# A delta-rule recurrence with a layer norm and a two-product MLP on one core: chunk 0 in two token halves, and mixed batches in the merged key product

## The chip, the cores and the metric

The kernel runs on one core of a Trainium2 chip. The metric is the device time of one execution in microseconds (us), smaller is better; a profiled execution also gives a trace, whose span runs from the first to the last instruction.

## The reference, cut to what matters

There are 4 batches, 8 heads, 768 tokens and a head size of 48, so the model width is 384, and the MLP is 1536 wide. The weights reach the kernel as 64-bit floats.

```
k_n = k / (norm(k) + 1e-6)
for t in range(768):                      # state is 48x48 for each batch and head
    y[t]  = q[t] @ state
    v_old = state^T @ k_n[t]
    state = state + beta[t] * outer(k_n[t], v[t] - v_old)
x   = y, heads joined: (4, 768, 384)
xn  = (x - mean) / sqrt(var + 1e-6) * g_ln
out = x + relu(xn @ w_ch1) @ w_ch2
```

## The kernel before, in words

**Chunks.** The 768 tokens are worked on in 12 chunks of 64. In a chunk the recurrence becomes a triangular system: G holds the key products K K^T, X is the inverse of a unit triangular matrix made of G and beta, and U = X V (V with the state's part taken off) are the values that are really written. Then y = (masked Q K^T) U + Q S, and the state S grows by K^T U. The inverse is made for blocks of 32 tokens on DVE (`rows_inverse` for pairs of chunks from 2 on, in 31 steps of a product and a subtraction, L1178 and L1185; `rows_near` for chunks 0 and 1, which works on blocks of 16 tokens, L1088 and L1095). For chunks 0 and 1 `near_join` puts two blocks of 16 together into one of 32: a transpose (L1135), a product on PE, a copy with a minus sign on ACT, a second product on PE (both L1140), and a predicated copy into X (L1147). The two blocks of 32 tokens of a chunk are joined in `recur`, by three steps of U on PE (L1256): the diagonal block of the first 32 tokens, the block below it, the diagonal block of the second 32. Between them stand a copy of U on ACT (L1266) and a subtraction on DVE (L1262).

**From y to the MLP.** For chunk 0, y of all 64 tokens is made after the third step (L1271), copied (L1312), its mean and variance taken on DVE (L1318, L1319), normalised (L1345 to L1351), turned on PE (L1383), and multiplied by g (L1399 on ACT, L1389 on DVE). The MLP of a chunk works on 256 rows: 4 batches by 64 tokens. Chunks 0 to 2 make the first product in the plain way: 12 groups (one for each 128 of 1536 columns) of 3 products, each two passes on PE with 256 columns (L1561), then a relu on ACT (L1570). Chunk 0's second product is plain too (L1583). Later chunks use schemes with fewer products: L1492 with 128 columns for the first one, L1664 with 192 for the second one.

**Weights.** Twelve pieces of 768 KB, six for each matrix, come as 64-bit words by DMA on the ACT queue (`fetch`) and are made 32-bit in four steps (`convert`): two on ACT (L798, L806), one on DVE (L803), one on POOL (L816).

**Merged key product.** From chunk 4 on, `gram_queries` makes the key products and the masked query products in one go, in two halves (`gram_half`, L1017), one for each bank pair. Each half has 32 products, two passes each, on array tiles of 64 rows by 32 columns. In a half all heads belong to one batch group g. In the column strip where the token block b equals g a product has 128 columns, in the other strip it has 64. ACT copies the diagonal blocks (L1030, three copies for a half) and the off-diagonal ones (L1042, two copies of 256 columns), and DVE masks the query part (L1035).

**Order.** Nothing runs in the order of the code. Each operation is a step with an engine, a cost, what it reads and writes, and a priority. A planner in the file runs through them and writes out one fixed order for each engine. What steers it are lists of numbers: `DUE` (one start and a slope for the MLP of each chunk or kind), `CAP` (latest times of the inverses), `T0` (earliest times of transfers) and `OFF` (one offset for each part of the program). PE is kept busy early on by products with zeros (L828, L1745).

Of the kernel before, what the change touches and what calls it, by code (L numbers as in the profile page):

```python
# [429 lines left out]
def kernel(  # L430
# [34 lines left out]
    UPER = 0.0076  # L465
    APART = 4
# [56 lines left out]
    pmask = sb("pmask", [128, 2, C])  # L523
# [3 lines left out]
    mask4 = sb("mask4", [128, BK], I32)  # L527
    lane = sb("lane", [128, 6])
# [25 lines left out]
    DUE = [-305.067857599, -184.157488926, 455.196580585, 43.3608971536, 325.931658715, 418.81557092, 734.822875439, 596.087521503, 954.313194593, 1226.15149798, 1753.77174886, 1187.43924725, -1.6924469742, 7.47712706956, 1.31274637377, 1177.34078649]  # L554
    CAP = [747.889715428, 1212.19696458, 1084.81830387, 1850.25080892, 1448.91733639, 908.561376039, 705.970562755, 575.226842462, 821.351411096, 750.46942201, 1687.9172189, 1227.4281115, 847.781737921, 881.489018474, 1102.45793961, 1447.53022967, 1091.57755388]
    T0 = [32.9830988769, 43.9377940451, 29.0921020937, 44.9281472705, 63.7206388166, 107.721780452, 109.01717894, 42.4201425188, 137.327678312, 9.9371017997, 7.55135349446, 21.1072922972, 47.3695615515, 3.2653345546, 12.003557196, 58.3820362978, 9.11313409582, 34.3183793157, 80.7294725245, 31.0940483985, 65.2240956281, 73.1210354066, 26.5270080195, 53.6799046277, 66.9289646085, 120.165225966]
    OFF = [-61.6829581914, -49.2365532767, -61.5532218662, 17.9216944294, -8.93066007944, -19.7935657519, -0.868007026628, 0, 8.96654600389, -13.8380038365, -50.331393939, -0.246849623501, -27.4676130541, 7.77550058171, -22.6886143688, -3.86879544818, -821.586638896, -2.38324144815, -18.1419009006, 5.55478119707, -0.273775179226, -4.22332705522, 80.7687098368, -5.39747372829, -20.4523790178, 62.9055142488, -7.43344176114, 31.9790263038, 21.8074958819, 8.7032008021, 8.84329072182, -13.4908722439, -14.3458640854, -21.0142536144, -8.17343430205, -9.08488196034, 3.21270803936, 29.7501729987, -370.210698155, 9.64783740174, -54.0771745917, 0, 6.02876528764, -18.715620035, -0.0266946289401, -157.574112514, 0.282239804554, -7.26929256528, -11.082495992, -8.27251668698, 6.02892269239, -13.9072145046, 0.152204562562, 22.7850900002, -47.5224937959, -1.16466857269, 2.33155240109, -49.6486518684, -51.2601416133, -62.465549245, -258.793504219, 1.2326483113, 35.4487428898, 31.3088385871, 11.2699410861, -113.147994473, 15.6085619425, -5.03125681565, -202.178096924, -25.0752772067, -0.665071753919, -6.77933533358, 3.23511675889, -68.4395072164, -60.5873923385, -42.4358792875, -97.9842212258, 12.0160900273, 18.6777945201, -900.573997296, -391.422008629, -20.8554491287, 12.9662458348, 1.75202460465, -24.9412070649, 4.97794129872, 75.9129714421, 9.69658805447, 5.43644995158, -526.886362328, -23.7620747742, 4.87077107518, 20.8620167161, 22.9095302211, -1.446032994, -2.31148664706, -2.833545276, 55.9003753723, 63.1638387207, -218.31594106, 287.768221191, 39.9673797514, 0, 804.43668455, 12.7893706811, 40.0678037528, 191.615596099, 0, 7.62314549532, 0, 51.2829387214, 28.4043993347, -5.30420927608, 18.5190140875, -7.64728420003, 7.63987656771, 61.2399462693, 717.489554984, 104.850886777, -30.443334038, -17.6796729001, 1.15630637025, 33.0836625929, 44.5914396091, 124.896962022, 76.2257084997, -17.2048186859, 9.19876963592, 11.8954016929, 17.6790867831, 26.5462796852, 8.59903556167, 24.5744786777, 48.2415672492, 84.1439987925, 573.112593574, -0.31404467451, 2.58380493428, 8.06139582684, -33.4691328586, -35.9526386931, -3.41549753963, 12.8997354829, -1.70472339012, -86.5639462817, 30.2317600188, 0.770084801705, 4.89412762855, 18.4175254922, -4.62459749441, -11.6877931109, 15.5755669109, -4.74496253875, 7.29402960805, -3.92469752656, -16.6201385477, -20.5867367042, 28.2665321084, 4.92853485667, 0, 15.3621971178, -8.42832996846, -56.587083905, 4.72501651567, -56.0564350712, -36.0703739182, 29.6200097296, 32.9003356762, -13.8377451749, 27.2835896047, -1.24739066499, 8.93640941449, 3.28676443186, 297.478212758, -19.9986109974, 45.0956057028, 0, -23.0001510965, 0, 36.6024183436, -9.30579353749, 11.8322652961, 15.1603515043, -21.1764521199, -3.23342658561, 10.9691701204, 0, -53.330288128, -6.9355981517, 35.7517193679, 17.1361544279, -16.5818223692, 7.98946302238, -5.9600414049, 135.238583305, 43.2173490845, 35.7070773331, 1504.57932506, -1.37439939367, 2.80197877523, 83.3684246786, -142.866519066, -50.2056045983, 97.2746589799, 0.00958371475404, 1.62790837443, -2.01014429694, 1.24356061286, 12.6149232043, -4.38744746062, -11.0164345418, -23.3392998149, -60.6068970653, -10.8042936204, -38.5434794118, 2.00080739243, -2.74074762392, -5.2820291742, -29.0236507323, 43.1273234385, 0.946905692554, -24.3700937813, 0, -21.7407793415, -12.5188513858, -23.5560537382, -50.7954370929, -3.45193559535, 15.4383131463, -11.5511037154, 16.3023360558, -25.1832177565, 16.2211956562, 10.4191918731]
# [102 lines left out]
    )  # L660
    SMALL = ["xor", "bits", "ma", "mb", "mc"]

    c_pool(lambda: nc.gpsimd.memset(pmask, 1.0), 0.2, ["pmask"])
    for e in range(2):
        c_pool(
            lambda e=e: nc.gpsimd.affine_select(
                out=pmask[half(e), 0], in_=pmask[half(e), 0], compare_op=ALU.is_gt, fill=0.0, base=0,
                pattern=[[1, C]], channel_multiplier=-1,
            ),
            0.3, ["pmask"],  # L670
        )
    for x in range(4):
        c_pool(
            lambda x=x: nc.gpsimd.affine_select(
                out=pmask[quad(x), 1], in_=pmask[quad(x), 1], compare_op=ALU.is_gt, fill=0.0, base=BK * (x % 2 - 1),
                pattern=[[1, C]], channel_multiplier=-1,
            ),
            0.3, ["pmask1"], r=["pmask"],
        )
# [317 lines left out]
    def gram_half(c, g, ps, pk, **kw):  # L997
# [5 lines left out]

        def segs(ap, step, n):
            return bass.AP(tensor=ap.tensor, offset=ap.offset, ap=[ap.ap[0], [step, 2], [1, n]])

        def prod():
            for j in range(NP):
                for hp, e in hp_e:
# [412 lines left out]
    def cap(i):  # L1422
        return CAP[i]

# [467 lines left out]
```

## Time and profile before

| what | us |
|---|---|
| runs shown | 531.07, 531.5, 535.16 (median 531.5) |
| the profiled execution | 531.07 |
| its span | 529.2 |
| PE busy | 501.5 (95% of the span) |
| DVE busy | 369.4 (70%) |
| POOL busy | 211.3 (40%) |
| ACT busy | 196.7 (37%) |

The profiled execution's own time is 1.9 us above its span. PE is the engine with the least idle time. The times of lines below are from the profiled execution; some records of matmuls are missing, so that a half of a merged product shows as, say, 39 of its 64 passes.

### The profile page before, as it was taken

The page shows a single profiled execution, that of the slowest core. Times are in us where ns is not written, and L with a number is a line of the kernel's source. Part 1 is how long each engine was busy: PE and PEld are TensorE (multiplying, and loading weights), DVE is VectorE, ACT ScalarE, POOL GpSimd, SP SyncE. Part 2 cuts the span into 40 slices and gives each one's busy share as a digit, 9 for nine tenths or more (in the row PEclk, how much of TensorE's full clock was granted, in tenths as well). Part 3 has the DMA queues.
Part 4 walks back from the last instruction along what each step waited for, and adds up shares of the span by engine and source line. Part 5 has one row for each costly group of instructions (what it writes and reads, how often), then busy time and mean ns, then how long its engine had stood idle before and what let it go on. Part 6 is the DMA issues. An engine that isn't in the chain of part 4 may idle for free.

```text
span 529.2 us, 22198 instructions
## 1 busy us (share of the span) xinstructions
PE 501.5 (95%) x9706; PEld 455.5 (86%) x9706; DVE 369.4 (70%) x849; ACT 196.7 (37%) x420; POOL 211.3 (40%) x320
## 2 busy tenths in 40 slices
PE   5967799999999999999999989999999999999996
PEld 3746677768898999989999879999889999999995
DVE  1899559997399866889895589895688893452331
ACT  2834875513812623525204522513523213242030
POOL 6151422236333560642724242452351815235352
PEclk8576779999999999999999999999999999999999
DMA  9965544365645445455311435221233010221101
GB/s 156 281 140 122 86 129 130 94 93 86 86 67 84 90 81 81 94 75 115 59 31 19 67 86 92 51 61 33 58 70 91 1 30 5 63 62 29 31 2 30
DMA packets 157457, 40.53 MB, mean 77 GB/s; under 512 B 150816, under 2 KB 153888, under 8 KB 157360
## 3 DMA queue, kind: packets, MB, share of 16 engines
q1 hardware_dynamic: 153520, 29.40, 31.4%
q10 hardware_dynamic: 3552, 9.63, 5.7%
q8 instruction: 76, 1.25, 1.0%
q0 software_dynamic: 288, 0.07, 0.1%
q14 instruction: 21, 0.17, 0.1%
HBM read 30.82 MB, written 8.26 MB: 74 GB/s over the span
## 4 chain that ended last, share of the span: by engine, by line
PE 86%; DVE 6%; issue 2%; DMA 2%; ACT 2%; SPq 1%; POOL 0%; DVEq 0%; ACTq 0%
PE f L1664 28%; PE f L1492 25%; PE f L1561 10%; PE two L1256 4%; PE f L1583 3%; PE by L1216 2%; PE two L1216 2%; PE by L1271 2%; PE two L1281 2%; PE two L1017 2%; DMA kr<-in_k_dram 1%; PE f L1140 1%; SPq L599 1%; DVE tmp L1088 1%; PE by L1017 1%
## 5 line engine op out<-in xcount | busy, mean ns | idle before, releaser
L1650 POOL TENSOR_TENSOR h_all<-h_all 128x256 f32<-128x256 f32 x99 | 73.9, 751 | 79.1 <-PE f L1664 65.9
L1664 PE MATMUL f<-w_sb,h_all 128*128 128x192 f32 x396 | 97.1, 333 | 1.4 <-ACT xln L1336 0.8
L1664 PE MATMUL f<-words,h_all 128*128 128x192 f32 x396 | 90.1, 329 | 0.0
L1492 PE MATMUL f<-xnt,w_sb 128*128 128x128 f32 x648 | 87.1, 277 | 0.4 <-issue 0.4
L1492 PEld LDWEIGHTS f<-xnt,w_sb 128*128 128x128 f32 x648 | 80.0, 192 | 1.6 <-ACT xnt L1377 0.9
L1664 PEld LDWEIGHTS f<-w_sb,h_all 128*128 128x128 f32 x396 | 66.3, 190 | 5.1 <-issue 2.3
L1515 DVE TENSOR_TENSOR h_all<-f,h_all 128x512 f32<-128x512 f32 (+1 forms) x90 | 49.5, 555 | 28.9 <-PE f L1492 19.8
L1664 PEld LDWEIGHTS f<-words,h_all 128*128 128x128 f32 x396 | 67.6, 190 | 1.1 <-ACT xln L1336 0.2
L1689 POOL TENSOR_TENSOR words<-h_all 128x128 f32<-128x128 f32 x66 | 32.8, 515 | 86.0 <-ACT h_all L1512 76.4
L1185 DVE TENSOR_TENSOR xb<-xb,tmp 128x31 f32<-128x31 f32 (+15 forms) x155 | 61.3, 396 | 4.0
L1178 DVE TENSOR_TENSOR tmp<-xb,gb 128x31 f32<-128x31 f32 (+15 forms) x155 | 60.0, 387 | 5.2 <-POOL xb L1164 1.0
L1561 PE MATMUL f<-xnt,w_sb 128*128 128x256 f32 x216 | 54.6, 399 | 1.2 <-issue 1.2
L1561 PEld LDWEIGHTS f<-xnt,w_sb 128*128 128x128 f32 x216 | 41.5, 198 | 8.2 <-issue 1.7
L1266 ACT COPY u<-two 128x768 f32<-128x768 f32 x24 | 19.2, 800 | 51.3 <-PE two L1256 43.8
L1492 PE MATMUL f<-second,w_sb 128*128 128x128 f32 x216 | 33.1, 276 | 1.7 <-POOL second L1472 1.7
L1512 ACT ACTIVATE h_all<-f 128x512 f32<-128x512 f32 (+1 forms) x36 | 17.4, 489 | 42.7 <-PE f L1492 31.0
L1682 DVE TENSOR_TENSOR o<-f,x 128x192 f32<-128x192 f32 x33 | 11.6, 352 | 30.5 <-PE f L1664 22.7
L1664 PE MATMUL f<-w_sb,words 128*128 128x192 f32 x132 | 32.1, 328 | 0.0
L1570 ACT ACTIVATE h_all<-f 128x256 f32<-128x256 f32 x36 | 13.7, 384 | 49.2 <-PE f L1561 49.0
L1492 PEld LDWEIGHTS f<-second,w_sb 128*128 128x128 f32 x216 | 29.2, 192 | 2.0 <-POOL second L1472 2.0
L1512 ACT ACTIVATE h_all<-h_all 128x512 f32<-128x512 f32 (+1 forms) x36 | 18.7, 521 | 29.4 <-DVE h_all L1515 29.3
L856 POOL TENSOR_TENSOR v<-v,knrms 128x768 f32<-128x768 f32 x10 | 15.3, 1533 | 30.4 <-PE f L1561 11.4
(194 smaller groups left out, 858.6 us busy)
## 6 DMA issues: line engine op xcount, KB each, us to landing
words<-in_moe_w_ch_dram ACTq DMA_DIRECT2D x8, 768.0 KB
out_dram<-o SPq DMA_DIRECT2D x48, 96.0 KB
xld<-xlt SPq DMA_DIRECT2D x9, 384.0 KB
xnt<-xld SPq DMA_DIRECT2D x36, 96.0 KB
tb<-in_q_dram SPq DMA_DIRECT2D x40, 64.0 KB
tb<-in_k_dram SPq DMA_DIRECT2D x32, 64.0 KB
v<-in_v_dram SPq DMA_DIRECT2D x8, 192.0 KB
w_sb<-in_moe_w_ch_dram ACTq DMA_DIRECT2D x2, 768.0 KB
```

Source lines behind the costliest of these rows:

```text
L1178: lambda j=j, n=n, w=w, t=t: nc.vector.tensor_tensor(out=t, in0=xb[:, 0:n, j : j + 1].to_broadcast([128, n, w]), in1=gb[:, j : j + 1, j + ...
L1185: "DVE", dve(n * w), lambda t=t, rest=rest: nc.vector.tensor_tensor(out=rest, in0=rest, in1=t, op=ALU.subtract),
L1216: nc.tensor.matmul(dst[half(e), hp, j], src[drows(hp), (e if n else key_half(c, hp, e)) * GP + j], s_all[drows(hp), e, j], start=(n == 0 o ...
L1256: nc.tensor.matmul(*args(e, e ^ hp, 2 * j + hp))
L1266: add("ACT", act(768), lambda: nc.scalar.copy(u_j, p_2), TWO, uk, after=["nought", *SMALL] if not c else (), **kw)
L1492: nc.tensor.matmul(wide(p[:, o : o + 128]), w[:, f : f + 128], r, start=start and m == n == 0, stop=stop, skip_group_check=True)
L1512: add("ACT", act(128 * m), lambda: nc.scalar.activation(to[0], p, ACTF.Relu), pk, to[1])
L1515: add("DVE", dve(128 * m), lambda v=ps(p): nc.vector.tensor_tensor(out=to[0], in0=v, in1=y[0], op=op), [*pk, *y[1]], to[1])
L1561: nc.tensor.matmul(p[:, 0:TOK], w1_sb[:, t, f * 128 : (f + 1) * 128], xnt[:, t], start=(t == 0), stop=(t == KC - 1))
L1650: add(eng, cost, lambda: e.tensor_tensor(out=out_, in0=x, in1=y, op=op), r, w, port=2 if eng == "Pool" else 1, pr=-2)
L1664: lambda f=f, t=start and f == 0: nc.tensor.matmul(p[:, 0:D2], lhs(f), rhs[:, f], start=t, stop=(f == F2 - 1), skip_group_check=True),
L1689: lambda f=f + i: e.tensor_tensor(out=s3[f], in0=one(0, 0)[0](f), in1=one(1, 0)[0](f), op=ALU.subtract),
```

## The change

Four things are changed, and two masks are added for them.

1. *Chunk 0 by token halves.* `near_join(0)` runs twice, once for tokens 0 to 31 and once for tokens 32 to 63, each with half of the passes and a mask of its own; the first goes to bank f2, the second to f3. After the first step of U and its copy, y is made from what U holds by then (`y0`), and the whole of the norm, now in a function `normed`, runs on it into the buffers of index 1 (x, statistics, normalised and turned rows), which hold right values for tokens 0 to 31. The recurrence goes on as before, and at its end y, norm and turn run again for all tokens into the buffers of index 0.
2. *First product of chunk 0 by token halves* (`first_mlp`): 12 groups for tokens 0 to 31 (from index 1), then 12 for tokens 32 to 63 (from index 0), each with 128 columns instead of 12 groups with 256. The relus are halved likewise.
3. *Mixed batches in the merged key product.* A half now takes both batch groups and half of the heads of each, so that products of 128 and of 64 columns meet in every column strip. Their number and sizes stay. The copies of the off-diagonal blocks become four of 128 columns for a half instead of two of 256.
4. *New order.* `DUE`, `CAP`, `T0` and `OFF` are all replaced, and the planner's own cost for a half of the merged product is lowered.

```
-        pe(128, lambda: prod(pe_, gf, xn, BK), ...
-        add("ACT", act(512), lambda: nc.scalar.mul(es, pe_, -1.0), FK[2], [ek], **kw)
-        pe(128, lambda: prod(pz_, es, xt), [ek, ("xd", c)], FK[2], 0.22, per=0.009, **kw)
+        for b in range(1 if c else 2):
+            quads = range(4) if c else (b, b + 2)
+            if b:
+                line.part += 1
+                pe_ = pz_ = f_[3].rearrange("p (h t) -> p h t", t=BK)
...
+            np, per = (128, 0.009) if c else (64, 0.0165)
...
+            if not c and not n:
+                line.part += 1
+                pe(64, lambda: out_y(range(GP)), [("pt", 0), *uk], BY, 0.65, name="y0", **kp_e)
+                normed(1, [(p_y, BY)] * 2, **kw)
+                line.part += 1
...
+    def first_mlp(n):
+        line.part += 1
+        for f in range(FT):
+            p, pk = bank()
+
+            def parts(t, n=n):
+                return t.rearrange("p (g i b) -> p g i b", g=2, b=BK)[:, :, n::2]
+
+            def first(f=f, p=p, n=n):
+                o = p[:, 0:128].rearrange("p (g i b) -> p g i b", g=2, b=BK)
+                for t in range(KC):
+                    nc.tensor.matmul(
+                        o, w1_sb[:, t, f * 128 : (f + 1) * 128], parts(xnts[1 - n][:, t], n), start=(t == 0), stop=(t == KC - 1)
+                    )
...
-            for j in range(NP):
-                for hp, e in hp_e:
-                    lk, lq = (((2 * x + g) * NP + j) * C for x in (key_half(c, hp, e), e))
-                    for b in range(2):
-                        o = ps[quad(2 * (e ^ hp) + b), hp, j * 2 * C : (j + 1) * 2 * C]
-                        if b == g:
+            for j in range(HP):
+                for r in range(2):
+                    for hp, e in hp_e:
+                        lk, lq = (((2 * x + r) * NP + HP * j + g) * C for x in (key_half(c, hp, e), e))
+                        for b in range(2):
+                            at = (r * HP + j) * 2 * C
+                            o = ps[quad(2 * (e ^ hp) + b), hp, at : at + 2 * C]
+                            if b == r:
...
         for e in range(2):
-            o, w = jn(goff[quad(2 * e + g), i])[:, :, hs], v[quad(2 * e + g), :, :, BK * (1 - g) : BK * (2 - g)]
-            add("ACT", act(256), lambda o=o, w=w: nc.scalar.copy(o, w), pk, [("go", i, e, x, g) for x in range(2)], **kw)
+            for r in range(2):
+                o = mine(jn(goff[quad(2 * e + r), i]))[:, :, HP * r : HP * r + HP]
+                w = v[quad(2 * e + r), :, HP * r : HP * r + HP, BK * (1 - r) : BK * (2 - r)]
+                add("ACT", act(128), lambda o=o, w=w: nc.scalar.copy(o, w), pk, [("go", i, e, x, r) for x in range(2)], **kw)
```

Of the earliest times (`T0`, rounded to whole numbers, in the planner's own us), these concern the front: the six pieces of the first weight matrix 8, 21, 47 (columns 0 to 767) and 3, 12, 58 (columns 768 to 1535) before, 29, 9, 25 and 1, 1, 42 after; the keys of chunk 2 44 before, 4 after; the values of chunk 1 29 before, 67 after; the queries of chunk 1 10 before, 48 after.

More of the change, by code (lines that the diff above doesn't have):

```diff
@@ L527 @@
     mask4 = sb("mask4", [128, BK], I32)
+    masks = [sb(f"mask{b}", [128, BK], I32) for b in range(2)]
     lane = sb("lane", [128, 6])
@@ L660 @@
     )
+    c_dve(
+        lambda: nc.vector.tensor_tensor(out=masks[1], in0=mask4, in1=mc, op=ALU.mult), 0.2, [("mask", 1)], ["mask4", "mc"], port=1,
+    )
+    c_dve(
+        lambda: nc.vector.tensor_tensor(out=masks[0], in0=mask4, in1=masks[1], op=ALU.subtract), 0.2, [("mask", 0)],
+        ["mask4", ("mask", 1)], port=1,
+    )
     SMALL = ["xor", "bits", "ma", "mb", "mc"]
@@ L1404, in recur @@
+        normed(c % 2, pys, **kw)
         if not c:
@@ L1553, in mlp @@
             return seven(c, hs, 33 * 0.43)
-        for f in range(FT):
+        if not c:
+            hs = list(range(FT))
+            first_mlp(1)
+        for f in range(FT) if c else ():
             p, pk = bank()
```

314 lines of the change are left out of this document (172 added, 142 removed).

## The prediction

> **What bounds the kernel now.** I read the busy shares first, then the table of stretches (start:end, length, busy us of PE, weight loads, DVE, ACT, POOL, then granted clock, DMA share, GB/s), then the chain that ended last, and last the rows of the lines that change.
>
> ```profile
> PE 501.5 (95%) x9706; PEld 455.5 (86%) x9706; DVE 369.4 (70%) x849; ACT 196.7 (37%) x420; POOL 211.3 (40%) x320
> ...
> PEclk8576779999999999999999999999999999999999
> ```
>
> ```profile
> 38.70:46.39 7.69, 4.40 (x133) 2.92 (x132) 7.00 (x27) 3.19 (x4) 1.79 (x2) 0.74 0.35 63
> 46.39:67.31 20.92, 16.32 (x544) 14.85 (x545) 13.24 (x31) 15.67 (x29) 7.05 (x7) 0.66 0.57 109
> 67.31:524.40 457.09, 452.05 (x8466) 416.47 (x8465) 323.01 (x706) 159.95 (x355) 184.91 (x277) 0.99 0.33 65
> ```
>
> From 67.31 on PE is busy for 452.05 of 457.09 us at full clock: after the front, time is PE work plus 5.0 us of gaps. Only two things can shorten it: less PE work, or an earlier start of the full stretch. Before 67.31 PE has gaps and a low clock. The chain shows what it does there:
>
> ```profile
> ...
> 56.60 2.15 issue
> ...
> 60.21 1.71 PE two L896 x62
> 62.15 0.88 issue
> 63.03 1.93 PE f L1140 x94
> 64.96 1.15 PE f L1561 x2
> 66.11 1.20 issue
> 67.31 4.42 PE f L1561 x10
> ...
> 81.40 0.81 PE two L1256 x64
> ...
> 130.49 1.07 PE two L1017 x39
> ...
> 399.27 13.40 PE f L1492 x120
> ...
> ```
>
> Two rows of PE's timeline (start, length, passes) stand for what the chain hides:
>
> ```profile
> 47.28 1.07 PE L1271 MATMUL by<-u,pt 64*64 64x48 f32 x32
> 48.14 1.92 PE L1281 MATMUL two<-u,kr 64*64 64x48 f32 x64
> ```
>
> The first product of the MLP (L1561) begins at 64.96, though chunk 0's rows were ready at 53.86 (L1389, 53.30 + 0.56). They came late, so their weights were left late too: the last early piece was issued on ACT's queue at 48.90 and its L816 ended at 60.89, 12.0 us later. What is to be seen is how slow PE is here: 10 passes of L1561 take 4.42 us, 0.442 each, where later 6 take 1.29 (0.2155 each); L1281 takes 1.92 and later 0.89.
>
> **Part 1 and 2, the front.** *When are the rows of tokens 0 to 31 ready?* U of the first step is copied by 39.57 (L1266, 38.77 + 0.80). `y0` has as many passes as both L1271 pieces, 1.11 + 1.07 = 2.2, so 41.8. From the first copy of y (47.57) to the last rows (53.86) it now takes 6.3 us. That gives 48.1, against 64.96 for the first L1561. Half joins cannot bring it much earlier: each array tile gets as many passes as before.
>
> *Are the weights there?* The columns needed first come from three pieces whose earliest times go from 8, 21, 47 to 29, 9, 25; the last of them by the 12.0 us above is ready at about 41. Price: the ACT queue now issues two other pieces at the start, beside the SP queue's keys of chunk 0 (landing 9.15, on the chain) and the keys of chunk 2, moved from 44 to 4. DMA is already full at 10 to 30 us (share 1.07 to 1.13). I take nothing for it, since 7 us lie between 41 and 48.1; if the landing at 9.15 itself slips, all of it counts, and I bound that by 3 us, about a third of its 7.5 us.
>
> *What is gained?* The 12 half groups are 72 passes of 128 columns: 72 x 13.40/120 = 8.0 us of PE work that can be done before the point that is now 67.31. Is there room? Idle is 20.92 - 16.32 = 4.6. Low clock costs, against the same counts later: two L896 about 0.7 each (against 1.08 of L1216), L1281 1.0, L1140 0.7 (against 1.22 at 55.13), the first two L1561 0.7, together 3.8; and 4.42 - 10 x 0.2155 = 2.3 behind 67.31. Room 10.7. New work in it: `y0` again, at full clock 0.94 (L1271 later), and six turns, 2 x 0.33 (L1383), 1.6 together. So 9.6 of 10.7 is used, and the start moves by 8.0 - 1.6 = **6.4**. Bounds: 0 (the start doesn't move) and 10.7 - 1.6 = 9.1.
>
> *Halving costs* 24 x 3 x 2 x 0.1117 = 16.08 against 72 x 0.2155 = 15.52: **+0.6**.
>
> *DVE* gets two norms (0.56 + 0.18 + 0.15 + 0.48 each), one L1389 (0.56), one L1147 (0.73) and two masks (0.24 each): 4.5 us where it is busy for 14.9 of 16.0 us (30 to 46). What goes back is `rows_near(1)`, whose steps end at 50.57, and with it the join of chunk 1. Its cover is 65.73 (L1147) to 81.40 (chunk 1's U): 15.7 us. Nothing is charged; without the cover it is 4.5.
>
> *ACT* gets two copies (0.48), two roots (0.29), three L1399 (0.37), one L1143 (0.60) and, for the first half, 12 relus (0.38, as L1030 for 128 columns): 7.8 us. In 46.39 to 67.31 it has 15.67 of 20.92, so 23.5 would be 2.6 too many. The conversions L798 and L806 at 56.88 to 58.74, four of 0.55, can go into the stretch before (ACT 3.19 of 7.69): 2.2 less. I charge **+0.4**. The relus are what empties the two banks in which half groups stand, so a relu behind the eight copies L907 (1.03 each) makes PE wait.
>
> The turn of `normed` is a wait added on PE: behind it stand the second join and two steps of U, and for them the rest of chunk 0. PE has fill products (L1745) there now, so up to the 1.2 + 0.7 us of these is covered.
>
> **Part 3, the merged product.** A half has 64 passes on 8 array tiles. At 13.40/120/128 = 0.87 ns a column, a tile in the busier strip works 8 x 128 columns = 0.89 us, in the other 0.45. The rows give about 1.0 for a half (1.07 above). Mixed, each tile has 4 x 128 + 4 x 64 columns, 0.67. With the same 0.11 on top it is 0.78, so 0.22 less for each of 16 halves: **-3.5**, and all of it counts since PE is 99% busy there. Bounds: 0.73 for a half, the shortest row for 64 small passes (L1256 from chunk 4 on), gives -4.3; 1.08, the longest (L1216), +1.3. I take -3.5, as the load of the tile is what changes.
>
> The Trainium skill speaks against this: "TensorE: Matmul & The Clock Gate", section "Wait — 56ns, not 53.3ns?", says that matmuls never start closer than about 25 ns apart, however short they are. By that, 64 passes would take 1.6 us in any mix and the part would bring nothing. The trace disagrees: the row of L1256 has 64 passes in 0.81 us, 12.7 ns each, so I give this little weight; with no gain here the sum would be 525.6.
>
> ACT pays for the mix: four copies L1042 more for a chunk at 0.37, 1.5 us, 11.8 over 8 chunks. ACT works 160 of 457 us there, and its copies (to 302.5 in the pair at 296) stand ahead of an inverse that is used later. Charged at nothing; without cover, 3.0 for a pair, four pairs 12.
>
> **Part 4, the new order.** No row prices it. Gaps of PE behind 67.31 are 5.0 us now. I bound it by -3 (2 us of gaps stay) and +15.8 (rival C), and take 0, as DVE (323 of 457) and ACT have room.
>
> **Sum** against the profiled execution: 531.07 - 6.4 + 0.6 + 0.4 - 3.5 = **522.2**; the median of the runs is 531.5, 0.4 above it. About 1% (5.3 us) is what a measurement can tell from no change here.
>
> **Rivals.** *A, the front keeps its start*: ACT or the banks hold the half groups back, or the order runs them only behind 67.31. For it speak ACT's 23.5 of 20.92 and the low clock; against it the free 5 to 8 us in the stretches before. PE then pays 1.6 + 0.6 and gains 3.5: 529.8.
>
> *B, the mix brings nothing*: passes are bound by something other than the tile. For it: L1216, with four tiles and 48 columns, takes 1.08 though its tiles work only 0.67. Against: L1256. 522.2 + 3.5 = 525.7.
>
> *C, slower: a chunk's rows come late.* From chunk 3 on, rows go from L1336 through DVE, out and back by DMA on SP's queue, and ACT to L1492. Now 298.46 to 314.21 is such a trip, 15.8 us, and PE idles only 2.6 in that stretch, as it has other products. `DUE` of chunk 1 goes to 806, so other products may be used up earlier. From 8.9 us uncovered the gains are eaten; a whole trip bare gives 522.2 + 15.8 = 538.0. Against it: one trip in nine shows, and for 1.7 us.
>
> *D, more than the sum*: the whole room is used, the mix reaches 0.73 and gaps shrink by 3: 531.07 - 9.1 + 0.6 - 4.3 - 3 = 515.3.
>
> **How the numbers follow.** Forecast 0.47 (its own range 518 to 526), A 0.15, B 0.11, C 0.16, D 0.11. Faster by over 1% means under 525.8 (526.2 from the median): nearly all of the forecast (0.46), D (0.11), half of B (0.05): 0.62. Slower by over 1%: C from 14 us bare, 0.15 of it. The rest, 0.23, is within 1%. The range goes from 513, below D by the 2 us of gaps that are left, to 535, which takes in A, B, a late first landing (525) and the lower half of C; some 0.12 of C and a little of D lie outside.
>
> **What would show it.** First product of chunk 0 starting at 47 to 52 and PE without gaps from about 61; clock full from there; L1017 0.75 to 0.85 for a half, 12.5 for all where it is 16; PE's gaps behind the front still about 5. The forecast is wrong if the first product starts late or stands in gaps behind relus, if a half stays at 1.0, or if a wait on rows (L1377's successors, POOL, ACT's L1336) over 5 us shows on PE.

## The result, and the profile after

The changed kernel takes 537.65 us in the median (534.65 to 540.36, 10 runs), the kernel before 531.29 us on the same chip (527.68 to 536.39, 10 runs): ratio 1.0124, 95% interval 1.0087 to 1.0161. The ratio leaves out one slow run of the kernel before (536.39 us). The forecast was 522.2, with a range of 513 to 535 and 0.62 for faster. Sign and range are wrong. The profiled execution after took 538.11 us (span 536.4), 7.0 us more than the one before. A second batch of runs on another chip gave 537.39 us and a ratio of 1.0159 (1.0131 to 1.0187). The experiments below ran on several chips; each one's ratio is to the kernel before on its own chip, and is read against this 1.0159.

The page of the kernel after (busy us, share, instructions):

```profile
PE 504.8 (94%) x9840; PEld 459.1 (86%) x9840; DVE 374.6 (70%) x861; ACT 203.6 (38%) x472; POOL 214.9 (40%) x320
```

The table of stretches after, at two of the bounds that the prediction used (start:end, length, busy us of PE, weight loads, DVE, ACT, POOL, granted clock, DMA share, GB/s):

```profile
46.39:67.31 20.92, 18.24 (x402) 15.75 (x400) 17.80 (x64) 16.73 (x35) 7.20 (x6) 0.84 0.82 191
67.31:524.40 457.09, 445.56 (x8711) 411.13 (x8710) 324.87 (x704) 164.79 (x398) 183.22 (x273) 0.99 0.31 59
```

No pass is missing from these two traces: the merged product has 1024 in each, 16 halves of 64, and a row of the chain with 39 shows a part of a half. The 134 passes that the kernel after has more are the second y (64), six turns and the halves (72), less eight fill passes.

Ahead of 67.31 PE now looks better: 18.24 busy of 20.92 (16.32 before) and clock 0.84 (0.66). Behind it, 11.5 us are gaps (5.0 before). The chain of work that ended last shows what stands there now; copies on ACT and the join of chunk 1 are in it where the kernel before had PE's first product:

```profile
38.06 1.69 PE f L1163 x58
39.91 1.16 PE two L1396 x56
...
64.29 1.03 ACT gdiag L923
...
72.77 1.93 PE f L1163 x128
```

PE's timeline after has the same events, from `y0` to the start of the early half, and at the join (start, length, passes, idle time before and what ended it):

```profile
42.94 2.04 PE L1286 MATMUL by<-u,pt 64*64 64x48 f32 x64
...
49.53 1.50 PE L1396 MATMUL two<-v,xt 32*32 32x48 f32 x64 [2.68 <-DVE v L1402]
...
55.95 1.11 PE L1418 MATMUL two<-u,kr 64*64 64x48 f32 x64
56.99 2.30 PE L1594 MATMUL f<-xnt,w_sb 128*128 128x128 f32 x18
...
72.77 1.93 PE L1163 MATMUL f<-xt,pt 32*32 32x32 f32 x128 [2.86 <-ACT pt L1177]
74.63 4.21 PE L1594 MATMUL f<-xnt,w_sb 128*128 128x128 f32 x18
```

The early half of the first product begins at 56.99, not at 48.1. At 72.77 PE waits 2.86 us inside chunk 1's join, and then 18 passes take 4.21 us, 0.234 each; at 87.95, with the clock at 1.00, 24 such passes take 2.94, 0.122 each.

The waits of PE that the profile lists from 46 to 92 us come to 6.4 us after, all of them for DVE or ACT. Before they came to 5.5 us, and 4.2 of these were the three gaps that the prediction's chain shows as "issue" (2.15, 0.88, 1.20), where the profile names nothing that PE waited for. So waits for data grew from 1.3 to 6.4 us.

**Where the 7 us stand.** To compare the two traces over time I gave every PE pass the spacing that its kind has at clock 1.00 (0.112 us for 128 columns, 0.216 for 256, 0.163 for L1664 and L1734, 0.0127 for a pass of U, and so on) and summed what was still to be done at a given time. The table shows how much more the kernel after has left than the kernel before, in us, in both of its profiled runs.

| time, us | 30 | 70 | 80 | 200 | 240 | 260 | 280 | 400 | end |
|---|---|---|---|---|---|---|---|---|---|
| after | 2.2 | -1.6 | 2.7 | 5.1 | 5.1 | 8.8 | 9.8 | 5.4 | 7.2 |
| after, second run | 2.2 | -0.7 | 3.5 | 7.3 | 7.3 | 9.3 | 10.4 | 5.4 | 6.8 |

The 2.2 at 30 us is the added work (y twice, six turns, the halves), as forecast (1.6 + 0.6). At 70 us the early half has put PE ahead. Between 70 and 80 that is lost, between 240 and 260 2 to 4 us more, and from 280 to 400 some come back. The ten runs of the kernel after lie 5.7 us apart, so a row of a single execution is read for its place, not for its last us.

### The profile page after: what moved, and what is told of

The parts are those of the page before. It is cut to its first block, busy times and chain, and to the rows that moved or that the text cites. A ratio compares the mean times of both kernels' runs of the same rounds, so it can differ in the third digit from the quotient of the medians.

```text
span 536.4 us, 22520 instructions
## 1 busy us (share of the span) xinstructions
PE 504.8 (94%) x9840; PEld 459.1 (86%) x9840; DVE 374.6 (70%) x861; ACT 203.6 (38%) x472; POOL 214.9 (40%) x320
## 4 chain that ended last, share of the span: by engine, by line
PE 63%; DVE 18%; SPq 6%; ACT 5%; DMA 4%; issue 3%; POOL 1%; DVEq 0%; ACTq 0%; POOLq 0%
PE f L1533 23%; PE f L1734 23%; SPq L601 6%; DVE tmp L1212 4%; DVE xb L1219 4%; PE two L1396 4%; DMA kr<-in_k_dram 2%; PE by L1250 2%; PE f L1163 2%; PE f L1631 2%; ACT gdiag L923 2%; PE two L1250 1%; PE by L1286 1%; DVE kq L892 1%; PE two L1418 1%
## 5 line engine op out<-in xcount | busy, mean ns | idle before, releaser
L1734 PE MATMUL f<-w_sb,h_all 128*128 128x192 f32 x396 | 96.9, 333 | 0.6 <-DVE o L1752 0.5
L1734 PE MATMUL f<-words,h_all 128*128 128x192 f32 x396 | 87.4, 328 | 0.1
L1759 POOL TENSOR_TENSOR words<-h_all 128x128 f32<-128x128 f32 x66 | 31.5, 494 | 139.4 <-ACT h_all L1553 100.4
L1533 PEld LDWEIGHTS f<-xnt,w_sb 128*128 128x128 f32 x648 | 80.5, 192 | 5.8 <-ACT xnt L1361 4.3
L1734 PEld LDWEIGHTS f<-w_sb,h_all 128*128 128x128 f32 x396 | 66.0, 190 | 3.5 <-issue 1.4
L1734 PEld LDWEIGHTS f<-words,h_all 128*128 128x128 f32 x396 | 67.6, 190 | 1.0 <-ACT h_all L1553 0.3
L1212 DVE TENSOR_TENSOR tmp<-xb,gb 128x31 f32<-128x31 f32 (+15 forms) x155 | 61.2, 395 | 4.1
L1219 DVE TENSOR_TENSOR xb<-xb,tmp 128x31 f32<-128x31 f32 (+15 forms) x155 | 60.4, 390 | 4.0
L1631 PE MATMUL f<-xnt,w_sb 128*128 128x256 f32 x144 | 35.6, 387 | 0.3 <-ACT h_all L1640 0.3
L1734 PE MATMUL f<-w_sb,words 128*128 128x192 f32 x132 | 32.5, 332 | 0.1
L1631 PEld LDWEIGHTS f<-xnt,w_sb 128*128 128x128 f32 x144 | 26.2, 190 | 4.9 <-ACT h_all L1640 1.0
L1752 POOL TENSOR_TENSOR o<-o,words 128x192 f32<-128x192 f32 x22 | 13.3, 622 | 36.6 <-DVE words L1752 29.2
L892 DVE STREAM_TRANSPOSE kq<-tb 128x256 f32<-128x256 f32 (+2 forms) x34 | 23.3, 718 | 5.7 <-DMA tb<-in_q_dram 3.7
L1752 DVE TENSOR_TENSOR o<-f,x 128x192 f32<-128x192 f32 x33 | 11.6, 350 | 22.3 <-PE f L1734 18.8
```

Source lines behind the costliest of these rows:

```text
L892: "DVE", 0.18 + 1.035e-3 * n, lambda o=o, w=w: nc.vector.transpose(o, w), tb_keys(i, "blk"),
L1212: lambda j=j, n=n, w=w, t=t: nc.vector.tensor_tensor(out=t, in0=xb[:, 0:n, j : j + 1].to_broadcast([128, n, w]), in1=gb[:, j : j + 1, j + ...
L1219: "DVE", dve(n * w), lambda t=t, rest=rest: nc.vector.tensor_tensor(out=rest, in0=rest, in1=t, op=ALU.subtract),
L1533: nc.tensor.matmul(wide(p[:, o : o + 128]), w[:, f : f + 128], r, start=start and m == n == 0, stop=stop, skip_group_check=True)
L1631: nc.tensor.matmul(p[:, 0:TOK], w1_sb[:, t, f * 128 : (f + 1) * 128], xnt[:, t], start=(t == 0), stop=(t == KC - 1))
L1734: lambda f=f, t=start and f == 0: nc.tensor.matmul(p[:, 0:D2], lhs(f), rhs[:, f], start=t, stop=(f == F2 - 1), skip_group_check=True),
```

## Experiments

Two theories were there at first. *Order*: the new order on the queues loses what the parts gain. *Parts*: the added pieces cost more than they bring. Later ones are named where they come up. In a kernel "in the order of" another one, the planner's start times are replaced, step by step, by those of the other, and steps that would stand ahead of what they need are pushed behind it:

```
     line.schedule()
+    START = [...]
+    for s_ in line.steps:
+        s_.start = START[s_.n]
```

The kernels with a whole list of this kind, apart from the last two, lack three fill products at the start; at 30 us PE has as much left as in the kernel they are made from.

**The mixed merged product** (both ways: taken out of the kernel after, put alone into the kernel before, each in its own order).

```
-            for j in range(NP):
-                for hp, e in hp_e:
+            for j in range(HP):
+                for r in range(2):
+                    for hp, e in hp_e:
```

> The changed kernel in its own order, step for step, but with the merged key product as it was: each half takes one batch group, and the off-diagonal copies are two of 256 columns again (their places in the order stay). Theory: the mix gains on PE what the profile of the changed kernel shows, a half takes about 0.9 us instead of 1.0, so 16 halves give back 1.5 to 2.5 us: this kernel takes 539 to 540 where the changed one takes 537.6, and PE's rows of the product go from 15 to 17 us. Rival (the mix costs, by its twice as many copies on ACT): this kernel is faster than the changed one, 534 to 537.

> The kernel before in its own order, step for step, with only the merged key product mixed (each place of an off-diagonal copy of 256 columns now issues two of 128). Theory: part 3 alone gains 1.5 to 2.5 us, 529 to 530 against 531.3, and the halves take about 0.9 us. Rival: twice the copies on ACT hold an inverse or a relu up, and it takes 531 to 533.

Measured: a_unmixed 537.43 us, ratio 1.0160 (1.0130 to 1.0189); b_mixed 530.60, ratio 1.0025 (1.0006 to 1.0044). The mix brings nothing. From its first pass to the first pass of the next step a lone half took 1.06 and 1.08 us of PE before; in the kernel after it takes 1.00. A pair takes 1.84 (from 178.58 to 180.42) where it took 1.96 (178.82 to 180.78). PE is busy with all 16 halves for 16.9 us in the kernel before, 16.2 in b_mixed and 15.7 in the kernel after. PE's timeline at a lone half, before and then after (a row's length runs to the end of its last pass, so it is a little over the spacing):

```profile
141.61 1.15 PE L1017 MATMUL by<-kq 48*32 48x64 f32 x64
142.69 0.59 PE L1664 MATMUL f<-w_sb,h_all 128*128 128x192 f32 x2
```

```profile
146.56 1.07 PE L1037 MATMUL by<-kq 48*32 48x128 f32 x64
147.56 0.76 PE L1734 MATMUL f<-words,h_all 128*128 128x192 f32 x3
```

The 0.7 us that b_mixed wins on PE up to 340 us is waited away by 360: at 400 it has exactly as much left as the kernel before.

**Single waits in the kernel after.** In a_join ScalarE does chunk 1's copy and two relus ahead of the copies for chunks 2 and 3; in a_xld SP issues chunk 5's load of turned rows ahead of query and key loads; a_all has both and a front in which the first U step, y and the norm stand ahead of the second half of the join and of the conversions.

```
+    MOVED = {393: 62.985, 358: 62.986, 356: 62.987}            # a_join
+    MOVED = {1103: 221.36, 1556: 221.37, 1553: 221.38, ...}    # a_xld
+    for s_ in line.steps: s_.start = MOVED.get(s_.n, s_.start)
```

> The changed kernel with one thing moved on ACT's queue: the copy with a minus sign of chunk 1's join, and two relus, now stand ahead of the last diagonal copy and the four off-diagonal copies of chunk 2. Theory (the new order, not the halves, loses the front's gain): the wait of 2.9 us inside the join at 70 us goes to under 1, and the cold passes behind it (18 in 4.2 us) get faster: 533.5 to 535.5. Rival (the halves themselves cost; the wait is only where the loss shows): the wait comes back as another one within 30 us and the time stays at 537 to 538.

> The changed kernel with five transfers moved on SP's queue: the outward transfer of chunk 5's normalised rows goes ahead of five of eight query loads, and the four that bring them back ahead of five key loads. Theory (rows came late because of their place on the queue): PE's wait of 3.1 us at 241 goes, 534 to 535.5. Rival (PE runs into another lack there, such as the inverse on DVE): the wait moves by some 10 us and the time is 537 to 538.

> The kernel after with three repairs of its order at once: ScalarE copies of chunk 1's join ahead of chunk 2 and 3 copies, the load of chunk 5's turned rows ahead of query and key loads, and chunk 0's first U step, y, norm and first groups ahead of the second join half's products and of ScalarE's conversions. 'Order': the front gains 2 to 4 us of the 6.4 that were forecast, and with the other two (about 0.7 and 1.5 us when alone) the ratio is 1.003 to 1.008. Rival 'bound elsewhere': what is won ahead of 80 us is given back at the next chunk, ratio 1.011 to 1.015.

Measured: a_join 536.75, ratio 1.0149 (1.0122 to 1.0175); a_xld 536.02, 1.0154 (1.0118 to 1.0191); a_all 545.37, 1.0283 (1.0231 to 1.0335). None is better than the kernel after by more than its interval. In a_join the join's one wait of 2.9 us became four gaps of 0.7 to 2.1 us in and behind the join (1.27, 0.69, 2.09 and 1.50). In a_all the early half does start 7 us sooner, and nothing is won:

```profile
50.11 1.57 PE L1594 MATMUL f<-xnt,w_sb 128*128 128x128 f32 x12 [1.66 <-DVE xnt L1373]
51.62 0.88 PE L1396 MATMUL two<-v,xt 32*32 32x48 f32 x64
...
76.65 1.59 PE L1163 MATMUL f<-pt,second 32*32 32x32 f32 x128 [2.25 <-DVE pt L1158]
```

What was moved behind it is late instead: the third step of U starts at 51.62 (49.53 in the kernel after), and chunk 1's join at 76.65 (68.32). At 90 us this kernel has 11.0 us more left than the kernel before.

For a_xld the place is seen on four rows of SP, DVE, POOL and ACT after. The turned rows are ready at 229.89; SP reaches their load at 233.08, behind eight query loads, and issues the loads back at 239.32:

```profile
227.91 5.07 SPq L601 DMA_DIRECT2D tb<-in_q_dram  x8
...
229.31 0.58 DVE L1346 STREAM_TRANSPOSE xlt<-xln 128x384 f32<-128x384 f32 x1 [1.08 <-ACT xln L1321]
...
233.08 0.44 SPq L601 DMA_DIRECT2D xld<-xlt  x1
...
239.32 2.62 SPq L601 DMA_DIRECT2D xnt<-xld  x4
...
243.87 1.31 ACT L1361 ACTIVATE xnt<-xnt,g_sb 128x256 f32<-128x256 f32 x3 [7.13 <-DMA xnt<-xld]
```

PE's wait in the kernel after:

```profile
244.43 0.71 PE L1533 MATMUL f<-xnt,w_sb 128*128 128x128 f32 x4 [3.09 <-DVE xb L1219]
```

The row puts the wait down to DVE's L1219, a step of an inverse, which these passes don't read. What they read comes from L1361 on ACT, and the first of its three parts (from 243.87, about 0.44 us each) ended just ahead of PE's 244.43. In a_xld ACT starts on the rows at 239.92, and PE still waits 1.4 us, until 242.09, just behind DVE's L1752, which empties a bank of the second product at 241.99 (241.64 + 0.35). So another wait seems to have taken the place of part of the first one.

**Order against parts.** Four kernels set the two apart: two that change over to the other order at 80 us, and two with one kernel's parts in the other's order throughout.

> The kernel after, with its own order of steps on every queue up to 80 us; every step that it had not issued by then follows in the order in which the kernel before issues it (the halves and the mixed merged product stay). Theory 'order': PE's remaining work in the kernel after is 2.7 us behind the kernel before at 80 us and 7.2 behind at the end, so 4.5 us of the loss come after 80 us from the new order on the queues; this kernel then ends about 2.5 us over the kernel before, ratio 1.004 to 1.006. Rival 'parts': what the changed parts themselves add (smaller copies of the merged product on ScalarE, PE passes) makes the later loss, whatever the order: ratio 1.011 to 1.015 as for the kernel after.

> The kernel before, with its own order and front up to 80 us, and every later step in the order of the kernel after; none of the changed parts is in it. 'Order': the later order costs its 4.5 us with the old parts too, ratio 1.007 to 1.010. 'Parts': no loss, ratio 0.999 to 1.003.

> The kernel before, all its steps in the order of the kernel after from the start (the whole first product stands where the kernel after has the second half of it; join, first chunk and merged product whole and unmixed). 'Order': as slow as the kernel after or slower, ratio 1.012 to 1.025, since it has the order's loss and not the early halves of the product. 'Parts': ratio 1.000 to 1.006, since the 2.2 us of PE work that the halves add are gone.

> The kernel after's parts (two half joins, y of the first tokens, halves of the first product, mixed merged product) in the kernel before's order of steps on every queue; what the change adds is put in where the kernel before has its neighbours, six half groups of tokens 0 to 31 ahead of the rest as soon as the weights are unpacked there (57 us), six more at 76 us. With x_old_parts_new_order this completes a table of four. Theory 'order': the parts cost little by themselves (2.2 us of added PE work, less what the early halves bring), ratio 0.999 to 1.006, and the rest of the loss belongs to the new order. Theory 'parts': ratio 1.010 to 1.018 whatever the order.

For the last one the groups of the first product had to be made in four calls, so that the six early ones of each half could stand first:

```
-    def first_mlp(n):
+    def first_mlp(n, fs=range(FT)):
...
-    first_mlp(0)
+    first_mlp(0, range(6))
+    first_mlp(1, range(6))
+    first_mlp(0, range(6, FT))
```

| ratio to the kernel before | old order | new order |
|---|---|---|
| old parts | 1 | 1.0198 (1.0155 to 1.0241) |
| new parts | 1.0347 (1.0308 to 1.0387) | 1.0159 (1.0131 to 1.0187) |

The two that change over at 80 us: h_new_then_old 542.71, 1.0231 (1.0191 to 1.0271); h_old_then_new 541.12, 1.0219 (1.0171 to 1.0267). All four are slower than the kernel before, and three lie above both ranges that were expected (x_old_parts_new_order lies in that of 'order'), so neither theory holds alone. It seems that parts and order belong together, and that in an order made for the other parts something stands in front of what is needed next; in the last two the loss falls in the front: x_old_parts_new_order has 8.9 us more left at 100 us and 8.0 at the end, x_new_parts_old_order 13.3 at 100. How much of the 1.2 to 1.6% is order and how much parts can't be read from this table.

**A displaced inverse?** In the kernel after, the last step of chunk 1's inverse ends at 65.55 us on DVE (50.57 before); the unpacking of the weights and the second half of the join stand ahead of it in the queue. Its place was put back in a_inv, with a_xld's loads in a_inv_xld, and alone into the kernel before in b_late_inverse; only start times are changed (L957 to L1133, and the join behind them).

> The kernel after, with chunk 1's inverse of the 16-row blocks (L957, L963, L1091 to L1133) put back to where the kernel before has it on VectorE, ahead of the join's copies and among the unpacking of the weights, and chunk 1's join products put right behind it on TensorE. Theory 'displaced inverse': in the kernel after chunk 1's inverse ends at 65.4 us, in the kernel before at 51.1, because the early half of the first product pulled the unpacking of w1 and the second half of the join ahead of it on VectorE; then the join of chunk 1 is late, PE waits in it at 68 to 73 us with the clock down, and what the early half gains is lost. The inverse should end at 53 to 57 us here, the wait inside the join should be gone, PE should stand 2 to 4 us further on at 80 us than in the kernel after, ratio 1.003 to 1.009. Rival 'front full elsewhere' (ScalarE's copies and the halves' own work set the pace): ratio 1.011 to 1.016 as for the kernel after.

> The same, and chunk 5's load of the turned rows put ahead of the query and key loads on SP's queue as in a_xld. 'Displaced inverse' and 'late rows' together: 3 us from the front and 1.5 from the wait at 241 us, ratio 0.999 to 1.006. If both places only move the wait elsewhere: 1.010 to 1.016.

> The kernel before, with nothing of the change but the place of chunk 1's inverse and join on the queues, which is that of the kernel after (planned some 10 us later). 'Displaced inverse': ratio 1.006 to 1.012, with a wait of PE in front of or inside chunk 1's join at 65 to 75 us. Rival: the inverse had slack in the kernel before, ratio 0.999 to 1.003.

> The kernel after, unchanged, on the chip of these runs as a measure for them: ratio 1.009 to 1.016.

Measured: a_inv 550.88, 1.0407 (1.0379 to 1.0435); a_inv_xld 549.53, 1.0397 (1.0361 to 1.0432); b_late_inverse 530.51, 1.0014 (0.9994 to 1.0034). The theory falls. In b_late_inverse the inverse ends at 67.1 us, and the time is the same. In a_inv the inverse stands on DVE ahead of chunk 0's subtraction and norm, and PE waits 6.2 us, until 53.1, for the subtraction (L1402) before the third step of U. In b_late_inverse PE has almost nothing to do from 60 to 70 us:

```profile
60.00:70.00 10.00, 1.22 (x2) 0.50 (x2) 9.35 (x26) 9.83 (x14) 3.40 (x4) 0.60 0.23 42
...
290.00:400.00 110.00, 108.16 (x2583) 100.60 (x2575) 84.40 (x194) 40.88 (x92) 45.88 (x72) 1.00 0.32 65
```

```profile
70.73 1.93 PE L1140 MATMUL f<-pt,second 32*32 32x32 f32 x128 [7.10 <-DVE pt L1135]
```

It stands 4.4 us behind the kernel before at 80 us, and only 0.9 at the end. From 290 to 400 us PE is busy for 108.16 us, where the kernel before has 105.43: PE's waits there grow shorter when the front is late. So the kernel before forgives some 3.5 us of a late front. The kernel after has used this reserve up: in the same stretch it is busy for 108.79 already.

**ScalarE at 60 to 80 us.** ACT is busy for 8.91 and 9.75 of 10 us there in the kernel after. Six of the eight copies of chunks 2 and 3 went to VectorE (a_act, a_act_xld, and the kernel before as b_act), or all eight were cut to 1/8 (a_nocopy).

```
-                if b and c < SLAB:
+                if b and c < SLAB or (b and c == 2) or c == 3:
                     add("DVE", ..., nc.vector.tensor_copy(out=o, in_=w), ...)
```

> The kernel after with six of the eight copies L923 of chunks 2 and 3 on VectorE, whose rows are idle at 68 to 74 us, and the copies L927 ahead of the join's copy L1177; the rest of the order as it is. Theory 'ScalarE is full': ACT is busy for 8.91 and 9.75 of 10 us at 60 to 80, and PE waits there for its copies and relus; with 6 us taken off it the join's wait of 2.9 us shrinks to under 1, PE stands about 3 us further on at 80 us, ratio 1.006 to 1.011. Rival 'absorbed or bound elsewhere': ratio 1.012 to 1.017.

> The same with chunk 5's load of the turned rows ahead of query and key loads (a_xld). 'ScalarE is full' and 'late rows' together: ratio 1.002 to 1.009; if neither place sets the end: 1.012 to 1.017.

> The kernel before with the same six copies (L907) on VectorE, none of the change. ACT is busy for 9.62 of 10 us at 60 to 70 there and VectorE for 1.39. If ScalarE's copies bound the front in both kernels: 1 to 4 us faster than the kernel before, ratio 0.992 to 0.998. If they only fill cover: 0.998 to 1.002.

> The kernel after, step for step in its own order, with the eight copies L923 of chunks 2 and 3 cut to 1/8 of their columns (1.03 us each, some 6 to 7 us of ScalarE's 18.7 busy us at 60 to 80; gdiag is preset with a constant on GpSimd at 24 us instead). Theory 'ScalarE's copies hold chunk 1's join and the relus': the wait in the join (2.9 us) and the slow groups at 74 to 79 us go, 3 to 6 us less, ratio 1.004 to 1.010. Rival 'absorbed': what is won before 80 us is waited for later, ratio 1.012 to 1.017.

Measured: a_act 541.54, 1.0243 (1.0208 to 1.0279); a_act_xld 538.42, 1.0179 (1.0156 to 1.0202); b_act 531.63, 1.0043 (1.0017 to 1.0069); a_nocopy 536.51, 1.0128 (1.0093 to 1.0164). a_act doesn't answer the question: its ScalarE copies of the same bank waited for VectorE's, and the join's copy stood behind them:

```profile
72.26 4.08 DVE L921 COPY gdiag<-two 32x512 f32<-32x512 f32 x4
76.43 1.49 ACT L927 COPY goff<-two 32x256 f32<-32x256 f32 x4 [6.27 <-DVE gdiag L921]
77.94 0.60 ACT L1177 ACTIVATE pt<-f 128x512 f32<-128x512 f32 x1
```

a_nocopy frees ACT (busy for 6.11 of 10 us at 70 to 80, 9.75 in the kernel after), and PE isn't busier there than in the kernel after (6.99):

```profile
70.00:80.00 10.00, 6.52 (x272) 5.94 (x272) 2.83 (x6) 6.11 (x14) 2.62 (x2) 0.72 0.43 65
```

*What came in place of the wait.* In both runs that freed the join's copy on ACT, a_join and a_nocopy, PE's wait for that copy shrank to 0.7 us, but gaps of 3.4 and 2.8 us marked "issue" stand in the join instead. In a_join:

```profile
69.57 1.12 PE L1163 MATMUL f<-pt,second 32*32 32x32 f32 x109 [1.27 <-issue]
...
73.85 1.70 PE L1163 MATMUL f<-xt,pt 32*32 32x32 f32 x109 [2.09 <-issue]
```

These gaps agree in time with the arrival of PE's own instructions. The traces have a DMA queue of the kind "instruction" (q8) with 76 packets of 16 KB before, for 9706 passes and as many weight loads, so about 255 instructions to a packet. Such packets landed at 68.15 and 72.23 in a_join, and at 57.36, 61.61 and 66.02 in the kernel before; the gaps marked "issue" end 1.3 to 1.6 us behind them. In the kernel after one landed at 71.13, and the join's second product began 1.64 us behind it, at 72.77, where ACT's copy ended at 72.72 (72.12 + 0.60). So the copy and the instructions seem to have come at nearly the same time, and bringing the copy forward alone could win little. No run changed when instructions arrive, so this is read from times that agree and isn't shown as a cause.

**The early half itself.** a_no_early leaves out the matmuls and relus of `first_mlp(0)`; every other step stays in its place.

```
-                for t in range(KC):
+                for t in range(KC) if n else ():
```

> The kernel after, step for step in its own order, but the first product of tokens 0 to 31 and its 12 relus are left out (72 passes, 8.1 us of PE work at full clock, 3.4 us of ScalarE). Theory 'the early half stands in time that PE had anyway': the chain of chunk 0's second half and chunk 1 sets the front's pace, and leaving the early half out gains under 3 us, ratio 1.009 to 1.016. Rival 'the early half stands in the way on PE or ScalarE': it gains 6 to 8 us, ratio 0.998 to 1.004.

Measured: 539.38, ratio 1.0198 (1.0163 to 1.0234). This is above the range of the theory and far from that of the rival: taking 8.1 us of PE work and 3.4 of ScalarE away doesn't make the kernel faster. The table of stretches of a_no_early, and then of the kernel after:

```profile
60.00:70.00 10.00, 5.19 (x265) 4.45 (x263) 6.19 (x21) 8.92 (x14) 0.95 (x1) 0.90 0.92 185
70.00:80.00 10.00, 5.35 (x140) 4.67 (x140) 5.75 (x10) 8.48 (x16) 4.76 (x3) 0.50 0.40 62
80.00:90.00 10.00, 10.00 (x176) 9.71 (x176) 7.31 (x19) 2.22 (x8) 1.23 (x1) 0.74 0.09 11
```

```profile
60.00:70.00 10.00, 9.19 (x302) 8.32 (x300) 7.47 (x27) 8.91 (x15) 0.95 (x1) 1.00 0.95 216
70.00:80.00 10.00, 6.99 (x153) 6.46 (x153) 4.37 (x6) 9.75 (x20) 4.66 (x3) 0.66 0.50 81
80.00:90.00 10.00, 10.00 (x195) 9.64 (x195) 8.46 (x23) 4.07 (x15) 1.32 (x2) 1.00 0.15 16
```

PE simply idles where the early half stood. Chunk 1's U starts at the same time, in a_no_early and then after:

```profile
90.92 0.88 PE L1396 MATMUL two<-v,xt 32*32 32x48 f32 x64
```

```profile
90.82 0.88 PE L1396 MATMUL two<-v,xt 32*32 32x48 f32 x64
```

At 70 us a_no_early has 3.4 us less left than the kernel after, at 80 1.9 less, and at 90 0.1 more. From 80 to 90 PE is busy throughout in both, but at clock 0.74 in a_no_early and 1.00 in the kernel after. So the equal time hides some 2 us that a lower clock took back: the early half itself may cost about that much, not the 6 to 8 of the rival. Chunk 1's U began at 81.33 in the kernel before.

No kernel of these beats the kernel before: b_mixed and b_late_inverse are within 0.3% of it, b_act is 0.4% slower, and all others are 1.3 to 4.1% slower.

## Why the prediction was wrong

**The front, -6.4: the step that failed.** "So 9.6 of 10.7 is used, and the start moves by 8.0 - 1.6" takes every us of PE work done earlier as a us off the end. With the +0.6 and +0.4 it would have put the kernel after 5.4 us ahead at 80 us. The table has it 2.7 us behind (3.5 in the second run), which is the 2.2 of added work and 0.5 to 1.3 more: of the 8.0 us of work to be done early nothing was gained. The step would hold if PE's work set the time at which PE is fully busy. Two thirds of the early half (48 of 72 passes) did go ahead of chunk 1's join, and a_no_early shows that its place was nearly free. But the room closes by itself. What ends the front, as PE's waits show, is the chain of chunk 0's second half and of chunk 1, and that chain moved back: chunk 0's last rows from 53.86 to 62.99 (62.37 + 0.62), chunk 1's first join product from 55.1 to 68.3, its U from 81.33 to 90.82. So work won at 70 us (1.6) is missing at 70 to 80, where PE waits. Of the 4.6 us of idle time that the prediction counted as room, 4.2 were gaps marked "issue", and it did not ask what PE waited for there. That the slip comes from the added pieces in the in-order queues ahead of that chain (second half of the join, y, norm, turn, unpacking of w1 ahead of time) is what the rows suggest; no single one of them was shown to be the cause. Moving the inverse, the join's copy or the copies of chunks 2 and 3, or leaving the early half out, didn't bring chunk 1's U forward.

**The start, 56.99 instead of 48.1.** The chain of y was right in its pieces and lacked what stands between them in the queues. On PE both second join products come ahead of the first U step (39.5 instead of 37.2), eight turns L856 ahead of `y0` (2.05 us; 42.94), L1286 and L1418 ahead of the first group; on ACT conversions come ahead of the copies of y (47.94). The rows were ready at 55.15 (L1373, 54.59 + 0.56). The prediction named the second join as queued behind the turn; it stood ahead. Rival A, "the front keeps its start", is nearer to what happened than the forecast, though its 529.8 counted on the mix and on a front that only stays where it was.

**The mix, -3.5: wrong, rival B's size.** The load of the busier tile fell from 0.89 to 0.67 us in the sum; a lone half went from 1.07 to 1.00. So the busier tile's load isn't what sets the time of a half, and the 0.07 that was won was waited away again. What does set it isn't shown. The Trainium skill ("TensorE: Matmul & The Clock Gate", section "Wait — 56ns, not 53.3ns?") has the same outcome by a floor of about 25 ns between starts. That floor isn't what is seen: 64 passes in 1.00 us are 15.6 ns each, below it.

**The halves, +0.6, and the new work, 1.6: right.** Together 2.2, as the table has at 30 us.

**DVE and ACT.** The cover of 15.7 us was used up nearly whole: the inverse of chunk 1 ends 15.0 us later (65.55 instead of 50.57). By itself that costs nothing, as b_late_inverse shows in the old order, so charging nothing was right for the kernel before. ACT's +0.4 can't be checked alone; the 12 relus were priced at 0.38 each and took 0.28. a_nocopy says that ScalarE's copies alone aren't what holds the front: with most of their time gone the ratio was 1.0128, 0.3% under that of the kernel after, inside the intervals. The gaps that came in the place of the join's wait leave open whether the copies and PE's instructions hold it together.

**The new order, 0: too low, and rival C seen in part.** Behind 80 us the forecast had -3.5 (the mix) and 0; measured are 4.5 us more in the first profiled run and 3.3 in the second. PE's idle time from 80 us to the end grew from 9.8 us to 12.6 (11.3 in the second run). The largest gap is C's mechanism, the trip of a chunk's rows through SP's queue, though at chunk 5 and for 3.1 us, not for a whole trip. C's 538.0 is close to the 537.65 by chance, as its sum kept the gains of front and mix. Repairing the queue cut that wait to 1.4 us and brought no gain beyond the intervals.

**What stays open.** The traces put the loss at 70 to 80 and 240 to 260 us, less what comes back from 280 to 400, and they agree with each other. Which of the added steps makes chunk 1 late, whether PE's instructions hold its join, and whether an order exists in which the new parts don't lose, isn't settled: every order tried for them, other than their own, was the same or worse. Repairs of single waits and orders taken over from the other kernel were tried; a full new search for an order was not.

## What to carry to other kernels

Room on one engine is not time won: before you count work moved into a gap as a gain, find out what closes the gap, and ask whether that comes any earlier. A quick test is to leave the moved work out. If the time hardly changes, that work isn't what holds the kernel up; but compare the clock as well, since a PE that idles more may run at a lower one, as it did here. When a repair removes one wait and the time stays, look at what PE waits for next: two things can be late at the same moment. A hole at the start can be forgiven later where the kernel waits for something else, so a us at the front need not be a us at the end, in either direction; and a long tuned order suits its own steps, so a test that mixes two orders may mostly measure the mixture.

## What the runs showed of the hardware

Holes on PE went together with a lower clock. In a_no_early, 70 to 80 us, PE is busy for 5.35 of 10, the granted clock is 0.50, and six passes of 128 columns take 1.65 us; in the kernel after, at clock 1.00 (64.13 us), six take 0.94. The clock came back late: from 80 to 90 us PE is busy throughout in a_no_early, at 0.74.

Gaps on PE for which the profile names no cause agree with a DMA queue: the ones marked "issue" in the joins and in the kernel before at 56 to 68 us end 1.2 to 1.7 us after a packet of 16 KB on the queue of the kind "instruction" landed. They stand among short passes (128 passes of a join product take 1.2 to 1.9 us here), where a packet of about 255 instructions lasts only as long as one such product.

A copy of 32 x 512 elements out of the bank into gdiag takes 1.02 us on VectorE (4.08 for four) and 1.03 on ScalarE, so there VectorE was no faster than ScalarE. It is longer than VectorE's predicated copy of 128 x 512 (0.73 to 0.76) and ScalarE's copy of 128 x 512 (0.58 to 0.61, L861). Which property of the copy costs this isn't shown; ScalarE's copies of 32 x 256 (0.36, L927) take no longer than its operations on 128 x 256 (0.39, L1640).

And in b_late_inverse PE did 6.7 us less from 60 to 70 us than in the kernel before (1.22 busy against 7.92), and the whole took the same time within the interval.
